# Smaller pieces of w_in, prepared two steps ahead, in a float32 Fourier-mixing and hard-swish kernel

## The chip, the cores and the metric

The kernel runs on one core of a Trainium2 chip. The metric is the device time of one execution in microseconds (us). The kernel before takes 1949.23 us, the median of 5 runs (1947.43 to 1950.19).

The engines that matter are TensorE (PE: matrix products, and PEld: its weight loads), VectorE (DVE), ScalarE (ACT), GpSimd (POOL) and SyncE (SP). Each works through its own queue of instructions in order; they wait for each other through semaphores. POOL and SP also issue the transfers (DMAs).

## The reference

```
X = fft(x, axis=1); X = fft(X, axis=2); x = X.real    # x: 8 x 3008 x 256, float32
x = x.reshape(24064, 256)
h = x @ w_in                                           # w_in: 256 x 2048
g = h * clip(h + 3, 0, 6) / 6                          # hard swish
out = g @ w_out                                        # w_out: 2048 x 256
```

The inputs w_in and w_out arrive as 64-bit floats; the rest is float32.

## The kernel before

The eight batches are worked on in pairs. Stage 1 (`stage1_first` for the first pair) transforms along one factor of the sequence (3008 = 47 x 64) and sends its result to DRAM (`zd`); `load_g` brings it back as g, turned; stage 2 (`stage2`, and `spread` for one odd column) makes the tile q from it with the tables T. The second transform, along the 256 columns, is not done on q: it is folded into w_in, once, at the start. `fold_w_in` multiplies w_in by the transform's table C and leaves the result in W1 (with one row of it spread over all partitions as the columns of WN).

What follows is a long loop of steps, `steps`, numbered s. A step is a chunk of 256 columns of q times two of the 16 blocks of 128 hidden columns: blocks fc and fc + 8, so eight steps (fc = 0 to 7) make a chunk. A step consists of

- `mlp1`: the products u and v (PE, eight passes of 256 columns; four matmuls, of which each is two passes in float32), then s = u + qn * WN, u = s + v, v = v - s (DVE), two ReLUs (ACT) and two gates (DVE), which leave the tile a;
- `combine` (POOL): four sums of a's quarters, for a fast matrix scheme of seven products instead of eight;
- `mlp2`: the products with w_out's blocks G into the accumulators acc, fourteen passes. For the first chunk (s = 0 to 7) `mlp2_first` uses the plain eight products instead, of twice the length in four matmuls (eight passes of 512 columns), since G's mixed blocks aren't made yet.

The loop is in software pipeline order: u and v of step s + 1 (s + 2 from step 8 on) are issued before the products with w_out of step s. The tiles u and v come from one pool of three buffers (`ps_h`, tag "uv"), so the v of a step can start only when DVE has finished with the u of the step before.

The weights are prepared beside the first steps. They come in 16 pieces j of 128 x 512 numbers, loaded by POOL (`load_w`; the 64-bit numbers are read as integers). ACT cuts the exponent out (`exponent_a`, two instructions into PM), PE subtracts its two halves with a product in float16 (`exponent_b`, tile ex, two passes), ACT scales it (`exponent_c`); DVE makes the mantissa (`mantissa`, two instructions into top) and multiplies both (`join`, into wi for w_in, into G for w_out). The functions `head` (exponent_a, mantissa and the next load), `tail` (exponent_c and join) and `unit` group these.

The order of all this is written out by hand: what stands first in the program stands first in each engine's queue. Before the loop, pieces 0 to 3 (all of w_in that the first two steps need) are prepared and half of their columns folded; between the first u and v and the next, the other half is folded (`fold_now(0, 1)`, `fold_now(NWI // 2, 1)`). Pieces 4 to 7 are w_out's for steps 0 to 3; pieces 8 to 11 are the rest of w_in, 12 to 15 the rest of w_out. `third_step` and `fourth_step` (s = 2 and 3) carry pieces 8 to 14, and four half-folds, with them; DUE puts pieces 6, 7, 14 and 15 behind steps 0, 1, 4 and 5. Each w_in fold is eight passes of 256 columns on PE, an ACT copy to W1, and, for its column of WN, either eight tiny products (`pw`) and a copy, or two DMAs of 128 numbers each on SP's queue (line 659).

Of the kernel before, what the change touches and what calls it, by code (L numbers as in the profile page):

```python
# [58 lines left out]
def kernel(  # L59
# [149 lines left out]
    def bank(shape, name):  # L209
        if starting[0]:  # L210
            return ps_a.tile(shape, F32, tag="acc", name=name)
        return ps_d.tile(shape, F32, tag="d", name=name)
# [154 lines left out]
                    self.blocks[m][4:] = [(m, 0), (2 + m, 0)]  # L367

    def mlp1(ch, fc):
        gr, of, nq = ch.ck // 2, ch.ck % 2 * TB, ch.nq  # L370
        q, qn = ch.pr.q[gr], ch.pr.qn[gr]
        u = ps_h.tile([P, 2, TB], F32, tag="uv", name="u")
        v = ps_h.tile([P, 2, TB], F32, tag="uv", name="v")
        for blk, ps in ((0, u), (1, v)):

            r = slice(0, P - blk)
            for i in range(2):
                f = fc + i * NF
                nc.tensor.matmul(ps[:, i, 0:nq], W1[r, blk, f * P:(f + 1) * P], q[r, blk, of:of + nq],  # L379
                                 start=True, stop=True)  # L380
        s = spool.tile([P, 2, TB], F32, tag="s", name="s")
        for i in range(2):
            f = fc + i * NF
            nc.vector.scalar_tensor_tensor(s[:, i, 0:nq], qn[:, of:of + nq], WN[:, f:f + 1], u[:, i, 0:nq],  # L384
                                           op0=AL.mult, op1=AL.add)


        a = apool.tile([P, 2, 2, TB], F32, tag="a", name="a")
        t = spool.tile([P, 2, 2, TB], F32, tag="t", name="t")
        ch.a[fc] = a  # L390
        if ch.last:
            activate_last(a, t, s, u, v, nq)
            return
        nc.vector.tensor_tensor(u[:], s[:], v[:], op=AL.add)  # L394
        relu(t[:, 0], u[:], 1.0 / 6.0)
        nc.vector.tensor_tensor(v[:], v[:], s[:], op=AL.subtract)  # L396
        relu(t[:, 1], v[:], -1.0 / 6.0)
        gate(a[:, 0], t[:, 0], u[:])
        rev, tk, vk = (m.rearrange("p i (k n) -> p (i k) n", n=N2) for m in (a[:, 1], t[:, 1], v[:]))
        gate(rev[:, :, ::-1], tk, vk)  # L400
# [38 lines left out]

    def mlp2_first(ch, fc):
        a = ch.a.pop(fc)
        for h in range(2):
            if fc == 0:
                ch.acc[h] = ps_a.tile([P, 2, TB], F32, tag="acc", name="acc")
            for f in range(2):
                nc.tensor.matmul(ch.acc[h][:], G[:, (B11, B12, B21, B22)[2 * f + h], fc, :], a[:, :, f],  # L448
                                 start=(fc == 0 and f == 0), stop=(fc == NF - 1 and f == 1))
        if fc == NF - 1:  # L450
            ch.r = epool.tile([P, 2, 2, TB], F32, tag="r", name="r")
            for h in range(2):
                for m in range(2):
                    nc.scalar.mul(ch.r[:, m, h], ch.acc[h][:, m], (1 - 2 * m) / WS)

# [86 lines left out]

    NWI, NWO = FF // 512, NF // 2
    WB = 512
    PIECES = [("in", 0), ("in", NWI // 2), ("out", 0), ("out", 1), ("in", 1), ("in", NWI // 2 + 1)]
    PIECES = [(k, n, i) for k, n in PIECES + [("out", j) for j in range(2, NWO)] for i in range(2)]
    assert NWI == 4 and NWO == 4
    raw, difs, exs, fracs, w = {}, {}, {}, {}, {}  # L550

    STRAIGHT = (0, 1, 8, 9, 14, 15)
    NEXT = {0: 8, 1: 9, 4: 10, 5: 11, 6: 12, 7: 13, 8: 14, 9: 15}

    def load_w(j):
        kind, n, i = PIECES[j]
# [2 lines left out]
        st = pool.tile([P, 2 * WB], I32, tag=tag, bufs=bufs, name="st")  # L559
        o = st[:].bitcast(moe_w_in.dtype)  # L560
        if kind == "in":
            nc.gpsimd.dma_start(out=o, in_=moe_w_in[i * P:(i + 1) * P, n * WB:(n + 1) * WB])
        else:
            r = (2 * n + i * NF) * P
            nc.gpsimd.dma_start(out=o.rearrange("p (c j) -> p c j", c=2),
# [16 lines left out]

    def exponent_b(j):
        pm = [PM[j % len(PM)][:, i].bitcast(F16) for i in range(2)]
        if j in (5, len(PIECES) - 1):
            exs[j] = wpool.tile([P, WB], F32, tag="ex", bufs=2, name="ex")
            nc.vector.tensor_tensor(exs[j][:], pm[0], pm[1], op=AL.subtract)
            return

        h = starting[0] or (j % 2 == 0 and 8 <= j < 14)  # L590
        exs[j] = ps_h.tile([P, WB], F32, tag="uv", name="ex") if h else bank([P, WB], "ex")
        for i in range(2):
            nc.tensor.matmul(exs[j][:], E[:, i], pm[i], start=(i == 0), stop=(i == 1))

    def exponent_c(j):
        nc.scalar.activation(exs[j][:].bitcast(I32), exs[j][:], AF.Identity, scale=2.0 ** 23)

    def mantissa(j):
        st = raw.pop(j)
# [7 lines left out]

    def join(j):
        kind, n, i = PIECES[j]
        frac, ex = fracs.pop(j), exs.pop(j)[:]  # L610
        if kind == "in":
            o = wpool.tile([P, WB], F32, tag="wi", bufs=4, name="wi")
            nc.vector.tensor_tensor(o[:], frac, ex, op=AL.mult)
# [10 lines left out]
    def mix_w_out(j):  # L624
# [5 lines left out]
        tt(g[5], g[B22], g[3], op=AL.add)  # L630
        tt(g[2], g[5], g[B21], op=AL.subtract)


    def fold_w_in(n, h):

        nb = WB // 2
        cs = slice(n * WB + h * nb, n * WB + (h + 1) * nb)

        ps = bank([P, 2, nb], "wps") if starting[0] else spare[len(copies) % 2]
        for blk in range(2):  # L640
            for i in range(2):
                nc.tensor.matmul(ps[:, blk], C[:, i, blk * P:(blk + 1) * P],  # L642
                                 w["in", n, i][:, h * nb:(h + 1) * nb], start=(i == 0), stop=(i == 1))
        fs = range(cs.start // P, cs.stop // P)


        pw = ps_h.tile([P, nb // P], F32, tag="uv", name="pw") if h == 0 else None
        for f in fs if h == 0 else ():
            for i in range(2):
                nc.tensor.matmul(pw[:, f - fs[0]:f - fs[0] + 1], w["in", n, i][:, (f % (WB // P)) * P:(f % (WB // P) + 1) * P],  # L650
                                 C[:, i, D - 1:D], start=(i == 0), stop=(i == 1))

        def copy():
            nc.scalar.copy(W1[:, :, cs], ps[:])
            if pw is not None:
                nc.scalar.copy(WN[:, fs[0]:fs[-1] + 1], pw[:])
                return
            for f in fs:
                nc.sync.dma_start(out=WN[:, f:f + 1], in_=W1[P - 1:P, 1, f * P:(f + 1) * P])

        copies.append(copy)

    def load_t(gr):
        for b in range(2):
# [29 lines left out]
        t = T[r, b].rearrange("p g a k n -> p g (a k n)")  # L694
        nc.scalar.copy(t, Z[r].unsqueeze(1).to_broadcast([N2, NG, 2 * TB]))

    copies = []

    def head(j):
        exponent_a(j)
# [8 lines left out]
        exponent_c(j)  # L711
        join(j)

    def unit(j):
        exponent_b(j)
        if j + 1 < len(PIECES):
            head(j + 1)
        tail(j)

    def fold_now(n, *hs):  # L720
        for h in hs:
            fold_w_in(n, h)

    def copy_all():
        while copies:
            copies.pop(0)()


    def see(x):
        nc.gpsimd.tensor_copy(seen[:], x)  # L730
# [5 lines left out]
    for k, c in enumerate(ORDER):  # L736
        for part in range(2):
            fold(first, c, part, nc.vector)
        stage1_first(first, c)
        keep_awake(1)  # L740
        if k + 3 < NXC:
# [14 lines left out]
    for j in range(4, 8):  # L756
        load_w(j)

    head(0)
    exponent_b(0)  # L760
    keep_awake(1)
    head(1)
    tail(0)
    exponent_b(1)
    keep_awake(1)
    head(2)
    tail(1)
    exponent_b(2)
    fold_now(0, 0)
    head(3)  # L770
    tail(2)
    exponent_b(3)
    copy_all()
    tail(3)
    for i in range(2):
        stage2(first, 0, i)
    spread(first, 0)
    fold_now(NWI // 2, 0)
    copy_all()
    starting[0] = False  # L780
    spare = [ps_a.tile([P, 2, WB // 2], F32, tag="acc", name="spare") for h in range(2)]

# [52 lines left out]
        p, ck, fc = steps[s]  # L835
        return chunks[p][ck], fc


    DUE = [(6,), (7,), (), (), (14,), (15,), (), ()]
    head(4)  # L840
    mlp1(*chunk(0))
    exponent_b(4)
    head(5)
    tail(4)
    fold_now(0, 1)
    fold_now(NWI // 2, 1)
    copy_all()
    unit(5)


    def third_step():
        exponent_a(9)
        mlp1(*chunk(3))
        exponent_b(8)
        mlp2_first(*chunk(2))
        tail(8)
        head_b(9)
        exponent_b(9)
        tail(9)

    def fourth_step():
        mlp2_first(*chunk(3))
        head(10)
        head(11)
        exponent_b(10)
        exponent_b(11)
        fold_now(1, 0)
        tail(10)
        tail(11)
        head(12)  # L870
        head(13)
        copy_all()
        exponent_b(12)
        exponent_b(13)
        fold_now(NWI // 2 + 1, 0)
        tail(12)
        tail(13)
        copy_all()
        mlp1(*chunk(4))
        fold_now(1, 1)  # L880
        fold_now(NWI // 2 + 1, 1)
        head(14)
        copy_all()

    prev = None
    for s, (p, ck, fc) in enumerate(steps):
# [3 lines left out]
            f(*a)  # L890
        if s < NF:

            if s in (2, 3):
                (third_step if s == 2 else fourth_step)()
            else:
                mlp1(*chunk(s + 1))
                if s == NF - 1:
                    combine(*chunk(NF))
                mlp2_first(*chunk(s))
            for dst, src in later[2 * s:2 * s + 2]:  # L900
                nc.sync.dma_start(out=dst, in_=src)
            for j in DUE[s]:
                unit(j)

            if s == 5:
                see(chunk(s + 1)[0].a[s + 1][:, 0, 0, 0:1])
                mix_w_out(0)
                mix_w_out(1)
            if s == NF - 1:
                mlp1(*chunk(NF + 1))  # L910
        else:
            if s + AHEAD < len(steps):
                mlp1(*chunk(s + AHEAD))
# [99 lines left out]
```

## Time and profile before

| | |
|---|---|
| median of 5 runs | 1949.23 us |
| profiled execution, its time | 1948.63 us |
| its span | 1946.7 us |
| PE busy | 1927.9 us (99%) |
| PEld busy | 1658.0 us (85%) |
| DVE busy | 1439.2 us (74%) |
| POOL busy | 1416.1 us (73%) |
| ACT busy | 682.5 us (35%) |
| first u of the loop (line 379) | starts at 51.11 us |
| first product of mlp2 (line 468, s = 8) | starts at 119.55 us |

The span is the time from the first to the last instruction of the profiled execution. "Busy" is the time that at least one instruction of the engine is on record; for PE, whose matmuls overlap, a busy share of 99% does not exclude short waits. A row of the timeline gives the start, the length, the engine, the line, the operation, out<-in, the shapes and how many; what stands in brackets is the engine's idle time before it and what ended it. In the trace a matmul of float32 shows as two passes.

### The profile page before, as it was taken

What the parts mean: (1) busy time and instruction counts of PE and PEld (TensorE: products, weight loads), DVE (VectorE), ACT (ScalarE), POOL (GpSimd) and SP (SyncE); (2) the same over time, 40 slices, a digit from 0 to 9 for tenths busy, and PEclk for the clock granted to TensorE, in tenths of its full rate; (3) what the DMA queues carried; (4) which work ended last, traced back from release to release, by engine and by line L of the source; (5) the groups of instructions that cost most, each with busy time, mean ns of one, the idle gap of its engine ahead of it and who ended that gap; (6) DMA issues with size and microseconds to landing.
All of it is one profiled execution on the core that took longest, in us unless ns stands there. A gap on an engine that the chain in (4) does not pass through costs nothing.

```text
span 1946.7 us, 27925 instructions
## 1 busy us (share of the span) xinstructions
PE 1927.9 (99%) x9254; PEld 1658.0 (85%) x9254; DVE 1439.2 (74%) x2778; ACT 682.5 (35%) x1166; POOL 1416.1 (73%) x1620
## 2 busy tenths in 40 slices
PE   8999999999999999999999999999999999999998
PEld 4678888888998888888898888888899888888887
DVE  6877777777777777777787777777778777777777
ACT  5633333333333333333333333333333333333332
POOL 3078888887688887787678887878667667666765
PEclk9999999999999999999999999999999999999999
DMA  8531312211112132111111221222110101101000
GB/s 225 173 87 39 75 52 59 55 43 31 37 30 55 47 76 63 43 51 30 39 36 44 57 55 44 49 51 53 35 28 20 28 17 26 35 12 28 19 19 20
DMA packets 148959, 96.71 MB, mean 50 GB/s; under 512 B 117791, under 2 KB 131235, under 8 KB 148814
## 3 DMA queue, kind: packets, MB, share of 16 engines
q1 hardware_dynamic: 137482, 58.09, 12.5%
q0 software_dynamic: 10672, 36.67, 6.7%
q8 instruction: 73, 1.20, 0.3%
q14 instruction: 72, 0.59, 0.1%
q10 hardware_dynamic: 660, 0.16, 0.0%
HBM read 57.57 MB, written 37.32 MB: 49 GB/s over the span
## 4 chain that ended last, share of the span: by engine, by line
PE 93%; DVE 3%; DMA 1%; ACT 1%; issue 1%; SPq 0%; DVEq 0%; POOL 0%; ACTq 0%
PE acc L468 56%; PE v L379 16%; PE u L379 16%; PE ps L328 2%; PE ps L223 1%; DMA xt<-in_x_dram,IX 1%; DVE a L424 1%; PE acc L448 1%; DVE s L384 1%; ACT t L421 1%; PE spare L642 0%; DVE o L529 0%; DVE u L405 0%; ACT PM L581 0%; DMA T<-in_c_stage_dram 0%
## 5 line engine op out<-in xcount | busy, mean ns | idle before, releaser
L438 POOL TENSOR_TENSOR c<-a 128x512 f32<-128x512 f32 (+1 forms) x375 | 469.1, 1251 | 363.4 <-PE acc L468 307.4
L468 PE MATMUL acc<-c,G 128*128 128x256 f32 (+1 forms) x3008 | 696.9, 374 | 0.0
L421 ACT ACTIVATE t<-u,half 128x512 f32<-128x512 f32 (+1 forms) x384 | 260.8, 679 | 1143.2 <-DVE u L394 1064.2
L468 PEld LDWEIGHTS acc<-c,G 128*128 128x128 f32 x3008 | 565.4, 190 | 71.1
L384 DVE SCALAR_TENSOR_TENSOR s<-qn,WN,u 128x256 f32<-128x256 f32 (+1 forms) x768 | 330.4, 471 | 333.0 <-PE u L379 332.2
L468 PE MATMUL acc<-a,G 128*128 128x256 f32 (+1 forms) x2256 | 541.2, 375 | 0.0
L468 PEld LDWEIGHTS acc<-a,G 128*128 128x128 f32 x2256 | 421.4, 189 | 71.2 <-issue 17.6
L379 PE MATMUL v<-q,W 127*128 127x256 f32 (+1 forms) x1536 | 389.0, 375 | 2.4 <-DVE a L424 2.4
L379 PE MATMUL u<-q,W 128*128 128x256 f32 (+1 forms) x1536 | 388.1, 375 | 0.0
L424 DVE SCALAR_TENSOR_TENSOR a<-t,u 128x512 f32<-128x512 f32 (+2 forms) x448 | 264.0, 601 | 103.0 <-ACT t L421 98.9
L379 PEld LDWEIGHTS v<-q,W 127*128 127x128 f32 x1536 | 288.2, 190 | 42.2 <-DVE a L424 1.9
L379 PEld LDWEIGHTS u<-q,W 128*128 128x128 f32 x1536 | 285.7, 190 | 35.2 <-issue 0.5
L438 POOL TENSOR_TENSOR c<-a,c 128x256 f32<-128x256 f32 (+1 forms) x375 | 269.2, 718 | 29.4
L438 POOL TENSOR_TENSOR c<-c,a 128x256 f32<-128x256 f32 (+1 forms) x375 | 268.9, 717 | 29.4
L394 DVE TENSOR_TENSOR u<-s,v 128x512 f32<-128x512 f32 x352 | 245.0, 696 | 38.1 <-DVE s L384 1.8
L424 DVE SCALAR_TENSOR_TENSOR a<-t,v 128x512 f32<-128x512 f32 (+1 forms) x480 | 263.8, 566 | 0.2
L421 ACT ACTIVATE t<-v,half 128x512 f32<-128x512 f32 (+1 forms) x384 | 260.7, 679 | 0.6 <-PE acc L468 0.4
L396 DVE TENSOR_TENSOR v<-v,s 128x512 f32<-128x512 f32 x352 | 243.9, 693 | 0.0
L438 POOL TENSOR_TENSOR r<-w,e 128x256 f32<-128x256 f32 (+1 forms) x92 | 88.8, 987 | 3.6
L478 ACT ACTIVATE e<-acc 128x512 f32<-128x512 f32 (+2 forms) x184 | 83.4, 545 | 0.0
L529 DVE STREAM_TRANSPOSE o<-r 128x256 f32<-128x256 f32 (+1 forms) x192 | 72.5, 415 | 0.2
L438 POOL TENSOR_TENSOR w<-w,e 128x512 f32<-128x512 f32 (+1 forms) x46 | 57.5, 1251 | 3.6
(103 smaller groups left out, 777.8 us busy)
## 6 DMA issues: line engine op xcount, KB each, us to landing
out_dram<-o SPq DMA_DIRECT2D x747, 32.0 KB
zd<-z SPq DMA_DIRECT2D x48, 192.0 KB
g<-zd SPq DMA_DIRECT2D x36, 256.0 KB
xt<-in_x_dram POOLq DMA_DIRECT2D x21, 256.0 KB, 3.7
qn<-qd SPq DMA_DIRECT2D x19, 256.0 KB
st<-in_moe_w_in_dram POOLq DMA_DIRECT2D x8, 512.0 KB, 8.7
st<-in_moe_w_out_dram POOLq DMA_DIRECT2D x8, 512.0 KB, 6.0
xt<-in_x_dram POOLq DMA_DIRECT2D x17, 192.0 KB, 4.0
```

Of the source, the lines that this page charges most:

```text
L223: nc.tensor.matmul(ps[b][h * PB:(h + 1) * PB, 0:n], F[rows(b), 0:PB], y[rows(b), 2 * h:2 * h + n], start=True, stop=not last, skip_group_c ...
L328: nc.tensor.matmul(ps[:, blk, u * P:n].rearrange("p (b k) -> p b k", b=2), g[:, kk, blk * (P + 1):blk * (P + 1) + P], T[:, :, gr, blk, kk, ...
L379: nc.tensor.matmul(ps[:, i, 0:nq], W1[r, blk, f * P:(f + 1) * P], q[r, blk, of:of + nq], start=True, stop=True)
L384: nc.vector.scalar_tensor_tensor(s[:, i, 0:nq], qn[:, of:of + nq], WN[:, f:f + 1], u[:, i, 0:nq], op0=AL.mult, op1=AL.add)
L394: nc.vector.tensor_tensor(u[:], s[:], v[:], op=AL.add)
L396: nc.vector.tensor_tensor(v[:], v[:], s[:], op=AL.subtract)
L421: nc.scalar.activation(t, h, AF.Relu, bias=half[:], scale=scale)
L424: nc.vector.scalar_tensor_tensor(dst, t, 1.0, h, op0=AL.min, op1=AL.mult)
L438: (eng or nc.gpsimd).tensor_tensor(out, in0, in1, op=AL.add)
L468: nc.tensor.matmul(ch.acc[i // 2][:, i % 2, 0:ch.n], G[:, i, fc, :], mv, start=(fc == 0 and i % 2 == 0), stop=(fc == NF - 1), skip_group_c ...
L478: nc.scalar.mul(ch.e[:, k:i + 1, 0:ch.n], ch.acc[i // 2][:, 0:i + 1 - k, 0:ch.n], 1.0 / WS)
L529: nc.vector.transpose(o[:, 0:n // DH, h], ch.r[:, m, h, 0:n].rearrange("p (j i) -> p j i", i=DH))
```

## The change

The pieces of w_in become 256 columns wide, with both halves of the 256 rows in one piece (128 x 2 x 256), where they were 512 columns of one half. So one piece is enough for one fold, and four pieces (two of w_in, two of w_out) hold all that two steps need. The order of the pieces becomes in, in, out, out, four times.

Before the loop only two pieces of w_in are folded, one with `pw` and one with DMAs into WN; pieces 2 and 3 (w_out's first) have their exponents subtracted by DVE instead of PE; the first `exponent_a` stands ahead of the last `stage1_first`. In the loop `first_steps` (even s) and `second_steps` (odd s) replace the hand-written third and fourth step and DUE: steps 0, 2 and 4 each begin the preparation of the next four pieces and fold two of them, steps 1, 3 and 5 finish it. All later folds use DMAs for WN. `mlp1` is split into its products and `activate`; `mlp2_first` takes a list of halves, and half of each odd step's products with w_out (four of eight passes) stands behind the next step's u and v. Exponents of odd pieces are kept in the banks `spare` that the folds also use.

```diff
-    NWI, NWO = FF // 512, NF // 2
+    NWI, NWO = FF // 256, NF // 2
     WB = 512
-    PIECES = [("in", 0), ("in", NWI // 2), ("out", 0), ("out", 1), ("in", 1), ("in", NWI // 2 + 1)]
-    PIECES = [(k, n, i) for k, n in PIECES + [("out", j) for j in range(2, NWO)] for i in range(2)]
+    PIECES = [q for j in range(NWO) for q in [("in", j, 0), ("in", j, 1), ("out", j, 0), ("out", j, 1)]]
...
-    def mlp2_first(ch, fc):
-        a = ch.a.pop(fc)
-        for h in range(2):
+    def mlp2_first(ch, fc, halves=(0, 1)):
+        a = ch.a[fc]
+        for h in halves:
...
-        if j in (5, len(PIECES) - 1):
+        if j in (2, 3):
...
+        if starting[0]:
+            exs[j] = ps_h.tile([P, WB], F32, tag="uv", name="ex")[:]
+        elif j % 2 == 0:
+            exs[j] = bank([P, WB], "ex")[:]
+        else:
+            exs[j] = spare[1 if j % 4 == 1 else 0][:].rearrange("p i n -> p (i n)")
...
-    def fold_w_in(n, h):
+    def fold_w_in(j, spread_by_pe=False):
...
+        nc.scalar.copy(W1[:, :, cs], ps[:])
+        if pw is not None:
+            nc.scalar.copy(WN[:, fs[0]:fs[-1] + 1], pw[:])
+            return
+        for f in fs:
+            nc.sync.dma_start(out=WN[:, f:f + 1], in_=W1[P - 1:P, 1, f * P:(f + 1) * P])
...
+        if k == NXC - 1:
+            exponent_a(0)
         stage1_first(first, c)
...
-    head(0)
+    head_b(0)
     exponent_b(0)
     keep_awake(1)
+    exponent_c(0)
     head(1)
-    tail(0)
+    join(0)
+    keep_awake(1)
     exponent_b(1)
-    keep_awake(1)
-    head(2)
     tail(1)
+    exponent_a(2)
+    fold_w_in(0)
+    head_b(2)
     exponent_b(2)
-    fold_now(0, 0)
-    head(3)
+    exponent_a(3)
+    fold_w_in(1, spread_by_pe=True)
+    head_b(3)
+    exponent_b(3)
     tail(2)
-    exponent_b(3)
-    copy_all()
     tail(3)
     for i in range(2):
         stage2(first, 0, i)
     spread(first, 0)
-    fold_now(NWI // 2, 0)
-    copy_all()
...
+    exponent_a(4)
     mlp1(*chunk(0))
+    head_b(4)
+    head(5)
...
+    def first_steps(s):
+        j = 2 * s + 4
+        more = j < len(PIECES)
+        if s > 0:
+            mlp2_first(*chunk(s - 1), halves=(1,))
+        if more:
+            exponent_b(j)
+        uv = mlp1_products(*chunk(s + 1)) if s == 0 else None
+        if more:
+            exponent_b(j + 1)
+            tail(j)
+            tail(j + 1)
+            exponent_a(j + 2)
+        activate(*chunk(s + 1), *(uv or mlp1_products(*chunk(s + 1))))
+        mlp2_first(*chunk(s))
+        if more:
+            exponent_b(j + 2)
+            exponent_c(j + 2)
+            exponent_a(j + 3)
+            fold_w_in(j)
+            fold_w_in(j + 1)
+            exponent_b(j + 3)
+
+    def second_steps(s):
+        j = 2 * s + 4
+        if j - 2 < len(PIECES):
+            head_b(j)
+            join(j)
+            head_b(j + 1)
+            exponent_c(j + 1)
+            if j + 2 < len(PIECES):
+                head(j + 2)
+            join(j + 1)
+            if j + 3 < len(PIECES):
+                head(j + 3)
+            mlp2_first(*chunk(s), halves=(0,))
+            mlp1(*chunk(s + 1))
+            return
+        mlp1(*chunk(s + 1))
+        combine(*chunk(s + 1))
+        mlp2_first(*chunk(s), halves=(0,))
+        mlp1(*chunk(s + 2))
+        mlp2_first(*chunk(s), halves=(1,))
```

## The prediction

> **What bounds the kernel now.** I read the page first, then busy time by stretches, the chain of waits over the start, and the timeline from 37 to 121 us, since the diff touches nothing behind that. The page:
>
> ```profile
> span 1946.7 us, 27925 instructions
> ...
> PE 1927.9 (99%) x9254; PEld 1658.0 (85%) x9254; DVE 1439.2 (74%) x2778; ACT 682.5 (35%) x1166; POOL 1416.1 (73%) x1620
> ...
> PEclk9999999999999999999999999999999999999999
> ...
> PE 93%; DVE 3%; DMA 1%; ACT 1%; issue 1%; SPq 0%; DVEq 0%; POOL 0%; ACTq 0%
> ```
>
> PE bounds the whole, at full clock. By stretches (length, then busy time of PE, PEld, DVE, ACT, POOL, the clock, DMA share and GB/s):
>
> ```profile
> 51.10:66.30 15.20, 14.27 (x57) 10.00 (x57) 12.81 (x26) 10.59 (x18) 2.00 (x4) 1.00 0.83 274
> 66.30:81.80 15.50, 15.26 (x51) 8.04 (x49) 14.44 (x28) 11.58 (x19) 1.95 (x3) 1.00 0.67 206
> ...
> 120.00:196.00 76.00, 76.00 (x367) 66.19 (x366) 55.60 (x100) 24.39 (x41) 65.34 (x76) 1.00 0.19 48
> ```
>
> From 120 us on PE never waits; so whatever brings the first product of line 468 forward brings the end forward by as much. Before that PE does wait, and DVE is nearly as full. The chain of waits before the first u, then the timeline:
>
> ```profile
> 46.06 1.78 PE ps L328 x16
> 47.84 0.89 PE ps L339 x8
> 48.74 1.73 PE wps L642 x8
> 50.47 0.79 PE pw L650 x8
> ```
>
> ```profile
> 51.11 1.11 PE L379 MATMUL u<-q,W 128*128 128x256 f32 x4
> ...
> 60.49 2.84 PE L448 MATMUL acc<-a,G 128*128 128x512 f32 x6 [0.93 <-DVE G L619]
> ...
> 118.58 1.13 PE L379 MATMUL v<-q,W 127*128 127x256 f32 x4 [1.54 <-DVE a L424]
> ...
> 119.55 1.46 PE L468 MATMUL acc<-a,G 128*128 128x256 f32 x6
> ```
>
> The reader is to see: after stage 2 (lines 328, 339) PE still folds for 2.5 us before u; w_out's products wait for G at 60.49; and v waits at 118.58, as three uv buffers are in use. So the start has two parts: the time to the first u (51.11), and from there to line 468 (68.44).
>
> **Part A, up to the first u.** PE's last stage-1 work ends at 37.67 (the two passes of awake at 36.81, 0.43 each). Before, piece 0's PM begins on ACT only at 37.50, behind the last copies of z. After, it stands ahead of them; piece 0 lands at 33.28, ACT needs 0.70 each, and is free by 34.4, so PM is ready at 35.9, and the copy that waits for PE at 36.16 isn't held. On PE then: ex 0 (0.43) to 38.1; two awakes (0.86 each) to 39.8; ex 1 waits for its PM (ACT: exponent_c 0.59 from 38.3, PM 1.40 to 40.3) and ends at 40.6; two folds, 16 passes of 0.2155, 3.45, to 44.0; pw 0.81 to 44.85; stage 2 16 passes 1.78 and spread 0.89 (rows above) to 47.5, if g is there: it was at 44.69, and the stores and SP's issues ahead of it are unchanged. ACT in the same time: PM of pieces 2 and 3, copies 0.59 and 0.16, two exponent_c 0.60 each to 46.65, q's copy 0.59 to 47.25; it does not hold u. DVE's two added subtractions (0.68) lie beside the folds. First u: 47.5 for 51.11, **3.6 us** earlier. Ends: 2.5 (only fold and pw behind stage 2 vanish) and 4.0.
>
> **Part B, from u to line 468, work.** Before, in PE start-to-start times: eleven u and v pairs by 1.725 = 18.98; eight w_out steps by 3.435 = 27.48; ten exponents by 0.43 = 4.30; 48 fold passes = 10.36; two pw = 1.62; one half of stage 2 0.89. Sum 63.63 of 68.44, which leaves 4.81 of waits: 1.20 at 60.49, 0.52 at 75.63, 0.71 at 83.6 and 84.0 (exponents), 0.37 at 105.5, 1.82 at 118.58, 0.18 at two u. After: no pw (-1.62), two exponents more (pieces 5 and 15 went by DVE; +0.86): 62.87, **0.76 us** less. Splitting step s's products in two costs nothing: the same passes, other place.
>
> **Part B, waits.** The 4.81 have mostly no counterpart: G for step 0 is joined at about 47.6, 6 us before its use, at 53.75; half of step 7's products lie ahead of the u and v that waited 1.82. What is late next:
> - Piece 4. POOL issues it behind `seen`, as before (45.23), and the first piece then landed at 49.18. PM takes 1.40, to 50.65; PE has finished v at 49.2, and its ex needs 0.43: it waits 1.25. Behind this PM on ACT stand step 0's ReLUs, behind them DVE's gate (0.69, to 52.05), and the second v, which needs that u's buffer: 0.4. Piece 5's PM stands behind the ReLUs: 0.3. Later pieces have more than 6 us of slack.
> - Bank `spare`: the exponent of piece 7 needs the copy of the first fold, which stands on ACT behind a PM (1.40): 0.4.
> - WN by SP. After each pair of folds SP issues four DMAs, 0.6 each, ahead of the stores to zd and loads of T, which queue behind them now. SP has the time: one zd store took up to 2.56 us to issue and one load of T 1.79, but all that SP issued between 60.2 and 71.7 fits between two pairs of folds, 16 us apart. DVE's s of the next step is the instruction that waits; the rest of its activation is queued behind it on DVE, and ACT's ReLUs and two steps' products wait for that. The trace's semaphore records give the landing of such writes: 3.9 to 4.8 us after issue for the four at 57.67, beside loads of pieces; 2.0 to 3.1 for the four at 92.70, with none. For the first pair my count goes: u of step 2 at 63.6 on PE, the w_out half, two exponents and u of step 3 behind it, so PE wants the v of step 3 at 68.8. The first fold's copy ends at 61.4; the first write lands 4.84 later, at 66.25 (the third, which s also needs, 1.2 + 3.9 later); s to the release of u took 3.1 (93.01 to 96.13), so v starts at 69.35: 0.5. Later pairs have no loads beside them (pieces 14 and 15 are issued at about 64 and 65) and I take 2.5, which costs nothing. If all four of a set are equally late, the third decides, some 3.7 us are free and each us beyond costs one: 4.8 in all three sets, the slowest row, would cost 3.3.
>
> Sum 2.85, with 0.15 for single gaps of 0.1 **3.0 us** for 4.81: 1.8 less. Ends: 1.0 (piece 4 lands 1 us earlier, WN in 2.5) and 7.8 (pieces 2 us later, +2; WN at 4.8 in all three sets, 3.3 for 0.5).
>
> One rule speaks against this choice. The rows are the two sets of four just given. Of the Trainium skill, the page "DMA: Bandwidth & Descriptors" says in "Rules for kernel authors" that many small transfers should be coalesced, as under 64 KB it is mostly overhead that is paid; and "Anatomy of one DMA" has a fixed part of some 2.0 us. The change adds six DMAs of 512 B in the place of products. By the fixed 2.0 us, an estimate from that page, no set would cost anything: waits of 2.5, and 1942.5 us; by the slow row in every set it would be 1945.8. The trace agrees with the 2.0 only where no loads run.
>
> **Covers.** For two steps DVE has four mantissas (1.15 each), two joins of w_in (0.61), four of G (0.38), two activations (3.4 each): 14.1 us, against PE's 15.8 (2 x 1.725 + 2 x 3.435 + 4 x 0.43 + 3.45). ACT has 11.8. If DVE's work grew by 1.7 us a pair of steps, it would be the bound. POOL: the mixes of G run from 102.33 to 109.4, combine at 114.04; after, `seen` is released at about 99.5, so they end at 106.6, and combine's a comes at 109.5: covered. w_in's pieces have two rows of 2 KB per partition in place of one of 4 KB, like w_out's: 0.72 to issue for 0.54, four times ahead of the stage that waits, in the ends above.
>
> **Sum.** 3.6 + 0.76 + 1.8 = 6.2 us: line 468 starts at 113.3, the span is 1940.5. The profiled execution took 1948.63 for its 1946.7 (1.9 around it), the median of the runs is 0.6 above it: 1949.2 - 6.2 = **1943.0 us**.
>
> **Rivals.**
> - WN late (the other side). If the writes land 6 us after issue in all three sets, 3 x 2.3 = 6.9 less the 0.5 counted eats the gain: 1949.4; from 7.3 us on it is slower by 0.2% (1953.2). For it: SP's queue fills there, and 4.8 has been seen. Against: 2.0 to 3.1 without loads. Chance 0.06. A part of it, 4.8 everywhere (1945.8; 1947.8 with the pieces 2 us late as well): 0.08.
> - DVE becomes the bound in steps 0 to 5. For: 14.44 of 15.50 busy already; and at 104.52 two G joins took 1.84 for 0.75 while POOL mixed G. Were all four of a pair so slow, +2.2, DVE would need 16.3 for PE's 15.8; with one wait for PE more, 0.5, it is 1 us for each of three pairs: 1946.0. Against: POOL has nothing but loads to issue then. 0.10.
> - The gain is given back: something behind 120 us (POOL's combine, x's loads) keeps its time. 1948 to 1949.5. Against: PE's 76.00 of 76.00, and everything there is placed by steps. 0.06.
> - The forecast, waits of 1 to 4.5 us: 1941.0 to 1944.6. 0.70.
>
> **How the numbers follow.** 0.2% is 3.9 us, about what a measurement of this kernel can tell from no change; faster means below 1945.3. The forecast's 0.70 is faster, and half of the 0.18 of the two partial rivals, where only one or two of the three places are hit: 0.79. The other half and the gain given back: 0.15. Slower: 0.06. The range takes the forecast's low end and the partial rivals: 1940.8 to 1946.4.
>
> **What would show it.** Right: first u at 47 to 48, line 468 at 112 to 114.5, no pw but one, waits of PE on ACT's PM at 50 and of v on DVE's a at 69, none over 0.5 us at 112. Wrong: DVE's s waiting for a DMA to WN and PE for a in three places; PE idle before acc with DVE without a gap; line 468 early but the end not.

## The result and the profile after

| | before | after |
|---|---|---|
| median | 1948.0 us (48 runs, 1946.17 to 1952.73) | 1944.37 us (28 runs, 1941.83 to 1948.98) |
| ratio | | 0.9981, 95% interval 0.9976 to 0.9986 |
| profiled execution, its time / span | 1948.63 / 1946.7 us | 1943.18 / 1941.4 us |

The change saves 3.7 us (2.7 to 4.7 by the interval); the forecast was a saving of 6.2. The predicted time, 1943.0, lies 1.4 under the measured one; but it was counted from a median of 1949.23, and the larger set puts the kernel before at 1948.0.

The page after, the lines that answer to those shown of before:

```profile
span 1941.4 us, 27877 instructions
...
PE 1925.3 (99%) x9230; PEld 1656.0 (85%) x9230; DVE 1437.4 (74%) x2778; ACT 681.8 (35%) x1163; POOL 1417.3 (73%) x1620
...
PEclk9999999999999999999999999999999999999999
...
PE 94%; DVE 3%; DMA 2%; ACT 1%; issue 0%; POOL 0%; DVEq 0%; SPq 0%; ACTq 0%; POOLq 0%
```

PE is still the bound at full clock, with 24 passes fewer. The stretches after (length, busy time of PE, PEld, DVE, ACT, POOL, clock, DMA share, GB/s):

```profile
46.92:62.73 15.81, 14.54 (x54) 9.04 (x53) 13.66 (x26) 12.39 (x21) 4.30 (x7) 1.00 0.75 264
62.73:79.72 16.99, 15.77 (x57) 9.81 (x56) 14.78 (x30) 11.15 (x19) 1.88 (x3) 1.00 0.61 209
79.72:95.23 15.51, 15.51 (x58) 9.89 (x56) 12.66 (x24) 10.29 (x17) 0.00 (x0) 1.00 0.41 119
120.00:196.00 76.00, 76.00 (x370) 65.23 (x369) 55.17 (x100) 26.79 (x47) 66.19 (x77) 1.00 0.24 58
```

A pair of steps that also prepares weights takes 15.51 us of pure PE work (third line). The two pairs before it lose 1.27 and 1.22 us of PE. The timeline after names where:

```profile
46.92 1.03 PE L381 MATMUL u<-q,W 128*128 128x256 f32 x4
...
48.70 1.40 ACT L591 ACTIVATE PM<-st,bias 128x512 uint8<-128x512 int16 x2 [0.99 <-DMA st<-in_moe_w_in_dram]
...
49.51 0.38 PE L608 MATMUL ex<-PM,E 128*128 128x512 f16 x1 [0.69 <-ACT PM L591]
50.16 0.38 PE L608 MATMUL ex<-PM,E 128*128 128x512 f16 x1 [0.27 <-ACT PM L591]
...
60.58 0.59 PE L608 MATMUL spare<-PM,E 128*128 128x512 f16 x2 [0.25 <-ACT W L668]
...
66.51 0.48 DVE L390 SCALAR_TENSOR_TENSOR s<-qn,WN,u 128x256 f32<-128x256 f32 x1 [1.40 <-DMA WN<-W]
...
69.29 1.13 PE L381 MATMUL v<-q,W 127*128 127x256 f32 x4 [1.22 <-DVE a L430]
...
112.74 1.13 PE L381 MATMUL v<-q,W 127*128 127x256 f32 x4
113.71 1.03 PE L474 MATMUL acc<-a,G 128*128 128x256 f32 x4
```

First the exponent of piece 4 waits at 49.51 (ACT's PM had itself waited 0.99 for the piece), then the exponent of piece 7 at 60.58 (its bank, behind a fold's copy), then v at 69.29, behind a DVE that stood 1.40 us waiting for a write to WN. The wait of v at the end (118.58 before) has shrunk to 0.14. (This is start to start: from the start of one pass to that of the next, less what a pass takes when nothing waits. By this count a wait is some 0.16 us longer than the idle time in its brackets.)

An execution's whole time hides part of this, because the last product of stage 1 (line 278, plus 0.43 for its pass) ends at another time in every execution, as the loads of x land: 35.0 to 37.9 us in all profiles here but one. So I read three stretches, each from PE's starts: from the end of stage 1 to the first u, from there to the first product of mlp2 (line 474, 468 before), and from there to the end.

| kernel | stage 1 to u | u to mlp2 | mlp2 to end | median us | ratio (95%) |
|---|---|---|---|---|---|
| before, two profiles | 14.30, 14.31 | 68.44, 68.45 | 1827.17, 1827.19 | 1948.0 | |
| after | 10.68 | 66.79 | 1827.71 | 1944.37 | 0.9981 (0.9976 to 0.9986) |
| after_again | 11.18 | 66.66 | 1827.71 | 1944.86 | 0.9978 (0.9969 to 0.9987) |
| after_third | 10.84 | 66.50 | 1827.70 | 1944.11 | 0.9976 (0.9965 to 0.9986) |
| whole_steps | 11.14 | 70.77 | 1827.69 | 1946.93 | 0.9994 (0.9985 to 1.0003) |
| exponent0_back | 11.71 | 66.46 | 1827.68 | 1944.07 | 0.9981 (0.9972 to 0.9990) |
| need_order | 11.44 | 67.41 | 1827.70 | 1943.85, one run | |
| late_writes | 11.43 | 75.11 | 1827.34 | 1951.55 | 1.0019 (1.0009 to 1.0028) |
| first_columns_by_pe | 10.91 | 65.98 | 1827.36 | 1942.35, one run | |
| loads_before_seen | 12.89 | 66.92 | 1827.69 | 1944.83, one run | |
| first_columns_timed | 11.10 | 65.81 | 1827.34 | 1942.74 | 0.9966 (0.9952 to 0.9979) |
| third_column_by_pe | 11.16 | 65.14 | 1827.74 | 1942.47 | 0.9967 (0.9955 to 0.9979) |
| more_on_dve | 10.68 | 66.47 | 1827.23 | 1943.86, one run | |

By the means of the three profiles of the changed kernel (10.90, 66.65, 1827.71): 3.4 us saved before the first u, 1.8 from u to mlp2, 0.5 given back behind it: 4.7 us in all. The three comparisons by runs gave 3.7, 4.3 and 4.7.

### The profile page after: what moved, and what is told of

It is laid out like the page before. It is cut to its first block, busy times and chain, and to the rows that moved or that the text cites. A ratio compares the mean times of both kernels' runs of the same rounds, so it can differ in the third digit from the quotient of the medians.

```text
span 1941.4 us, 27877 instructions
## 1 busy us (share of the span) xinstructions
PE 1925.3 (99%) x9230; PEld 1656.0 (85%) x9230; DVE 1437.4 (74%) x2778; ACT 681.8 (35%) x1163; POOL 1417.3 (73%) x1620
## 4 chain that ended last, share of the span: by engine, by line
PE 94%; DVE 3%; DMA 2%; ACT 1%; issue 0%; POOL 0%; DVEq 0%; SPq 0%; ACTq 0%; POOLq 0%
PE acc L474 56%; PE v L381 16%; PE u L381 16%; PE ps L328 2%; PE ps L223 1%; PE acc L454 1%; DMA xt<-in_x_dram,IX 1%; DVE a L430 1%; DVE s L390 0%; ACT t L427 0%; DVE o L535 0%; DVE u L411 0%; PE spare L658 0%; DMA WN<-W 0%; DMA st<-in_moe_w_in_dram 0%
```

## The experiments

**The same kernels again.** after_again and after_third are the changed kernel, before_again the kernel before, without an edit.

> The changed kernel once more, for a second profile. The profiles say 5.3 us for the change (spans 1946.7 and 1941.4), the medians of the runs 3.6. Theory A (the sum of the prediction, of which the profile shows line 474 at 113.7 for 119.55): the runs give -3.5 to -5.5 us again, and the new profile has the first u 9.1 to 11 us behind the end of stage 1's last awake and line 474 66 to 67.5 us behind that u. Theory C (what lands late differs from execution to execution, and the profile caught a quick one): the second profile has the writes of WN or the pieces later, line 474 at 115 us or behind it, and says so in DVE's waits for DMA.

> The kernel before, once more, for a second profile and as a zero of the comparison. Theory A: within 0.5 us of the kernel before in the runs; the profile has the first u at 51 to 51.7 and line 468 68 to 69 us behind it. Theory C, that the first profile of before was a slow one: first u or line 468 1 us or more earlier than 51.1 and 119.55.

> The changed kernel again, beside the two that follow, for a comparison on one chip: 3 to 5 us under the kernel before (1944 to 1945.5), first u to first product of mlp2 66.6 to 66.9 us, and 1827.7 from there to the end, with DVE's gap of 0.46 us before the u of line 411 at its place 1347.9 us behind the first product of mlp2.

The places are those of theory A. The first product of mlp2 stands at 115.77 in after_again, which theory C forecast, but 1.7 of the 2.1 us lie in the end of stage 1 (37.93 for 36.24) and 0.5 in a wait for g; no write or piece came later. In before_again the first u stands at 49.80, again for stage 1, which ended at 35.49 instead of 36.81. before_again gave 1947.65 us, ratio 0.9998 (0.9989 to 1.0007): two sets of one kernel agree within the 0.1% of the interval. What is under 1 us can't be settled by medians here; the middle stretch, equal to 0.01 us in the two profiles of before and within 0.3 in three of after, can settle it.

**whole_steps: the products of a step kept whole.** The split that the prediction costed at nothing is undone; all else stays.

```diff
     def first_steps(s):
-        if s > 0:
-            mlp2_first(*chunk(s - 1), halves=(1,))
...
-            mlp2_first(*chunk(s), halves=(0,))
+            mlp2_first(*chunk(s))
             mlp1(*chunk(s + 1))
```

> The changed kernel with the products of w_out of every step kept together, ahead of the next step's u and v; pieces, folds and their order as after. The split moves 1.72 us of PE work (four passes of 512 columns) between a step's v and the use of what hangs on it. Theory A, in which I costed the split at nothing by itself but let it cover the u and v of steps 8 to 10, and DVE's and ACT's work beside odd steps: without it PE waits about 1 to 1.5 us in each of steps 1, 3, 5 and 7, together 3.5 to 4.5 us slower than after, that is about as fast as before. Theory B (the pieces and the shorter way to the first u carry the gain, the split is decoration): within 1 us of after.

Measured: 1946.93 us, and 70.77 us from u to mlp2, 4.1 more than the mean of after. PE's waits in the timeline of whole_steps, behind the places where after waits too:

```profile
85.04 1.13 PE L381 MATMUL v<-q,W 127*128 127x256 f32 x4 [0.61 <-DVE a L430]
101.43 1.13 PE L381 MATMUL v<-q,W 127*128 127x256 f32 x4 [1.48 <-DVE a L430]
116.18 1.13 PE L381 MATMUL v<-q,W 127*128 127x256 f32 x4 [1.54 <-DVE a L430]
```

Two pairs of u and v follow each other there with no w_out products between them, and the second v wants the buffer that DVE frees 3 us after it begins; start to start the three waits cost 0.78, 1.64 and 1.70. So half a step of products is the cover that these v need: the passes as such cost nothing, their place is worth 4.1 us, most of the 4.7 that the change brings by the stretches; the medians beside each other, 1946.93 and 1944.86 (after_again), show 2.1 of it. Theory A had the size, with four places where the trace has three. Two of the three waits have no counterpart in the kernel before: they belong to the order of the steps that the change itself brings, and the split covers them.

**exponent0_back: the first exponent behind stage 1 again.**

```diff
-        if k == NXC - 1:
-            exponent_a(0)
         stage1_first(first, c)
...
+    exponent_a(0)
     head_b(0)
```

> The changed kernel with the first cutting of an exponent put back behind the last copies of stage 1 on ScalarE. Theory A, Part A of the prediction: PM of piece 0 takes 1.40 us on ScalarE, and PE waits for it, less what awake passes hide: the first u 1.1 to 1.3 us later, and all of it carried to the end: 0.9 to 1.3 us slower than after. Rival: the first u waits for g (landed at 43.9 in the profile of after, where PE came to stage 2 at 44.16): then only what goes beyond g's landing counts, still 1.0. If something behind absorbs it (the wait for piece 4, 1.3 us in the profile of after, shrinks by the same), no change at the end: 0 to 0.3.

Measured: the first u comes 0.8 us later than the mean of after (11.71 behind stage 1), the middle stretch is 0.2 shorter, and the time is the changed kernel's, 1944.07. The first u and v in the timeline of exponent0_back:

```profile
48.97 0.79 PE L608 MATMUL ex<-PM,E 128*128 128x512 f16 x2
49.60 1.02 PE L381 MATMUL u<-q,W 128*128 128x256 f32 x4
51.61 1.13 PE L381 MATMUL v<-q,W 127*128 127x256 f32 x4 [0.98 <-DVE a L430]
```

The exponent of piece 4 no longer waits for its piece, but the second v waits for DVE in its place: start to start 1.45 us of waits remain up to the exponent of piece 5, of 1.61 in after (and the same 1.45 remain in loads_before_seen below). So the wait for piece 4 stands over one that is nearly as long, and an earlier piece alone would bring about 0.2. The earlier exponent is worth 0.8 before the first u, less than the 1.1 to 1.3 expected, and 0.6 in all, which medians don't show.

**need_order: the order of the writes to WN.**

```diff
-        for f in fs:
-            nc.sync.dma_start(out=WN[:, f:f + 1], ...)
+        if k == 1:
+            for f in (fs[0] - NF, fs[0], fs[1] - NF, fs[1]):
+                nc.sync.dma_start(out=WN[:, f:f + 1], ...)
```

> The four writes of a set go to WN in the order in which they are needed: the two columns of the next step (f and f + 8) first, then those of the step behind it. In the trace of the changed kernel the third write was issued at 61.72 us, DVE's s waited 1.40 us for it, and PE's v 1.39 us for DVE. Theory A (the third write of the first set is what v of step 3 waits for, a term that the prediction had at 0.5): the write that decides becomes the second, issued at about 61.1, so v waits about 0.8 in place of 1.39 and the stretch from the first u to the first product of mlp2 is 66.1 to 66.3 us (66.79 and 66.66 in the two profiles of the changed kernel). Rival B (all four land together, beside the loads, whatever their order): 66.6 to 66.8.

Measured: 67.41 us, over both expectations. The write that decides was issued at 61.01 instead of 61.72 (0.42 us earlier, counted from the first u), but DVE waited longer. The two halves of step 2's s, which reads the first two columns of this set, in the timeline of need_order:

```profile
64.57 0.48 DVE L390 SCALAR_TENSOR_TENSOR s<-qn,WN,u 128x256 f32<-128x256 f32 x1
66.86 0.48 DVE L390 SCALAR_TENSOR_TENSOR s<-qn,WN,u 128x256 f32<-128x256 f32 x1 [1.81 <-DMA WN<-W]
```

From issue to the s that it released the write took 5.85 us; the third writes of the three profiles of the changed kernel took 4.79, 4.56 and 4.45. Theory A falls here, and B's size is too small.

The semaphore records in the traces, from which the prediction read its landings, say why. In the ten profiles whose first fold leaves both columns to DMA, the write of this first set that SP issues first lands 1.92 to 1.96 us after its issue (in late_writes it is one into the unread tile); every later one of the set takes 4.43 to 7.58. In after the DMA share is 0.01 from 59.7 to 61.9 us and 0.83 from there to 66.5: the first write, issued at 60.56, is through at 62.49, and the others go out into the loads of the next pieces. The second place, to which this edit moved the column, is one of the late ones. That the loads are what holds the writes is read from these times; no run moves the loads away.

**late_writes: the same writes some 2.4 us later, in all three sets.**

```diff
+        if not starting[0] and k == 0:
+            for i in range(4):
+                nc.sync.dma_start(out=junk[:, i:i + 1], in_=W1[P - 2:P - 1, 1, cs.start:cs.start + P])
         for f in fs:
             nc.sync.dma_start(out=WN[:, f:f + 1], ...)
```

> Ahead of each later set of writes to WN, SP issues four more transfers of 512 B into a tile that nobody reads: the writes go out about 2.4 us later, three times. It leaves nothing out. Theory A (the prediction's count: the third write decides, the first set has no slack left, the other two have little, and beyond it a microsecond is a microsecond): 2.4 us at the first set; at the second, 78.39 + 2.4 + 2.3 to land, s 1.9 later than in the changed kernel, of which about 1.2 reach v; at the third about 1.8. Together 4.5 to 5.4 us: first u to first product of mlp2 71.3 to 72.2 us for 66.8, and a time like that of the kernel before, 1948 to 1950 us, DVE's s waiting for DMA in three places. Rival B (only the first set is near the path, the other two are hidden): 2.0 to 2.8 us, 69.0 to 69.5, and about 1947. Rival C (SP's queue is off the path): under 0.5 us.

Measured: 1951.55 us, slower than the kernel before (1.0019), and 75.11 us, 8.5 more than after. DVE's s that waits for the third write and the v of steps 3, 5 and 7 in its timeline, then the stretches around the first of them (columns as above):

```profile
70.36 0.48 DVE L390 SCALAR_TENSOR_TENSOR s<-qn,WN,u 128x256 f32<-128x256 f32 x1 [1.38 <-DMA WN<-W]
...
73.14 1.22 PE L381 MATMUL v<-q,W 127*128 127x256 f32 x2 [4.80 <-DVE a L430]
...
88.95 0.48 DVE L390 SCALAR_TENSOR_TENSOR s<-qn,WN,u 128x256 f32<-128x256 f32 x1 [0.73 <-DMA WN<-W]
...
91.73 1.13 PE L381 MATMUL v<-q,W 127*128 127x256 f32 x4 [0.28 <-DVE a L430]
...
105.04 0.48 DVE L390 SCALAR_TENSOR_TENSOR s<-qn,WN,u 128x256 f32<-128x256 f32 x1 [0.75 <-DMA WN<-W]
...
107.82 1.13 PE L381 MATMUL v<-q,W 127*128 127x256 f32 x4 [1.18 <-DVE a L430]
```

```profile
68.50:72.00 3.50, 0.00 (x0) 0.00 (x0) 2.01 (x4) 0.32 (x1) 0.00 (x0) 0.92 1.03 363
72.00:74.50 2.50, 1.36 (x3) 1.17 (x4) 2.35 (x5) 2.50 (x5) 0.00 (x0) 0.50 0.86 284
74.50:78.40 3.90, 3.90 (x7) 1.73 (x6) 3.64 (x7) 2.17 (x4) 0.00 (x0) 0.52 0.06 22
78.40:82.00 3.60, 3.60 (x14) 2.25 (x13) 1.94 (x6) 1.29 (x3) 0.00 (x0) 1.00 0.00 0
```

Start to start the three waits are 4.97, 0.44 and 1.35 us, against 1.19 (mean), 0 and 0 in after: 5.6 us, at all three places. That is theory A, a little over its 5.4, since the first set's third write went out 3.75 us later and not 2.4; B and C fall. Another 2.5 us are something else: after 4.80 us without work PE's clock was granted at half, and the passes up to 78.4 took twice their time. Of the remaining 0.4, 0.2 lies in the wait for piece 4.

The 3.7 us that the prediction called free, counted from the issue of a set's third write, nearly hold. In the first set of the three profiles of the changed kernel that write landed 4.77, 4.53 and 4.43 us after its issue and v waited 1.38, 1.15 and 1.05: 3.4 were free each time. In the two later sets of late_writes it landed 4.2 us behind the fold's second copy, right behind which it is issued in after, and v waited 0.44 and 1.35: 3.7 and 2.9 were free. But a quiet write takes 2.0 of them itself, and so little is left that some 2.4 us of SP's queue, lost three times, turn this change's gain into a loss, with the clock's 2.5 on top.

The trace also gives the landing at both loads of the queues, as the time from a write's issue to the s that waited for it. In the first set (DMA share 0.94, 298 GB/s) the two writes that s waited for took 5.23 and 4.89 us; in the other two (share 0.10, 1 GB/s) 2.15, 2.01, 2.16 and 2.05.

**first_columns_by_pe and first_columns_timed: two columns of WN by PE.** One edit in two runs. (The expectations name step 3 as the reader of these columns; it is step 2's activation that reads them, and v of step 3 that waits for the buffer it frees.)

```diff
-            for f in range(2):
+            for f in range(2 if starting[0] else 1):
...
+        if pw is not None:
+            nc.scalar.copy(WN[:, fs[0]:fs[0] + 1], pw[:, 0:1])
+            fs = fs[1:]
...
-            fold_w_in(j)
-            fold_w_in(j + 1)
+            fold_w_in(j, spread_by_pe=(s == 0))
+            fold_w_in(j + 1, spread_by_pe=(s == 0))
```

> The two columns of WN that step 3's activation needs first are made by PE with four tiny passes each, as in the kernel before, only in the first set of folds in the loop; the other columns go by DMA. Theory A (v of step 3 waits 1.39 us for nothing but these writes): that wait goes, PE works 0.8 us more: first u to first product of mlp2 66.1 to 66.4 us for 66.79 and 66.66. Rival B (behind the writes DVE's own work holds v nearly as long, for it is 14 us of every 16 busy): the wait stays over 0.7 us and the stretch becomes 67.0 to 67.6.

> The kernel of first_columns_by_pe, timed: the first two columns that step 3 needs by PE, the rest by DMA. Theory A (the wait for WN was 0.7 to 0.8 us of PE's time net of the eight tiny passes): first u to first product of mlp2 65.9 to 66.1 us, 0.6 to 1.0 us under the changed kernel in the median, and 0.36 more if DVE's gap far behind is absent again: 1.0 to 1.3 under it, about 1943.3. Rival B (one profile's luck): within 0.3 us of the changed kernel.

Measured: 65.98 and 65.81 us, and 1942.74 us. The wait at v is gone and 0.8 us of tiny passes are paid for it: the net 0.75 is theory A's size. Nothing else holds v there. The sum has one more term, though: the wait for the bank of piece 7's exponent (0.41, start to start) is gone too, as tiny passes now stand ahead of it.

**third_column_by_pe: only the column that was late.**

```diff
-            fold_w_in(j, spread_by_pe=(s == 0))
+            fold_w_in(j)
             fold_w_in(j + 1, spread_by_pe=(s == 0))
```

> Only the third column of the first set (f + 8, which the second half of step 3's s needs first) is made by PE, with four tiny passes; the column f goes by DMA as in the changed kernel, where it was issued at 60.56 and s did not wait for it at 64.64. Theory A (the write that was late is the third alone): no wait for WN, 0.4 us of PE's work less than in first_columns_by_pe: first u to first product of mlp2 65.5 to 65.7 us, 1.1 to 1.6 us under the changed kernel. Rival B (the first write is on its edge too, it lands up to 5 us after its issue beside the loads): s waits for it up to 1 us at 64.6, the stretch is 65.9 to 66.6.

Measured: 65.14 us, 1.5 under the mean of after, and 1942.47 us. DVE in the timeline of third_column_by_pe, steps 2 and 3:

```profile
63.90 0.87 DVE L390 SCALAR_TENSOR_TENSOR s<-qn,WN,u 128x256 f32<-128x256 f32 x2
68.78 0.87 DVE L390 SCALAR_TENSOR_TENSOR s<-qn,WN,u 128x256 f32<-128x256 f32 x2
```

No s waits for WN, and the four tiny passes stand where PE waited 0.41 us (start to start, in after) for the bank of piece 7's exponent, a wait that is gone too. Some 0.2 of the 1.5 is not the edit's: piece 4 happened to be waited for 0.67 us here, for 0.85 to 0.94 in the three profiles of after. This version is 6.2 us under before by medians and 1.6 under the changed kernel beside it. The two intervals (0.9955 to 0.9979 and 0.9965 to 0.9986) overlap, so that last step is carried by the stretches, which are those of one profile.

**loads_before_seen: pieces 4 and 5 loaded ahead of the wait for g.**

```diff
+    load_w(4)
+    load_w(5)
     see(first.g[0][:, 0, 0:1])
-    for j in range(4, 8):
+    for j in range(6, 8):
         load_w(j)
```

> POOL issues the loads of pieces 4 and 5 ahead of the instruction that waits for g, in place of behind it. In the changed kernel the exponent of piece 4 and v behind it cost PE 0.86 + 0.43 us of waiting at 49 us, as ACT waited 0.99 us for the piece. Theory A (the wait is the late issue's and nothing else): first u at its place behind stage 1 (10.7 to 11.2 us behind the end of stage 1's products), and from the first u to the first product of mlp2 65.4 to 65.8 us for 66.79. Rival B (the megabyte of the two pieces shares the queues with z's way to DRAM and back, so g comes later): first u 11.7 to 13 us behind stage 1, with PE waiting for g ahead of stage 2, and the sum of both stretches the same as in the changed kernel or longer (77.5 us and more).

Measured: the wait for piece 4 is gone, and the first u comes 2.0 us later; both stretches together take 79.8 us for 77.6. PE in the timeline of loads_before_seen:

```profile
45.56 2.02 PE L328 MATMUL ps<-T,g 128*128 128x128 f32 x16 [2.08 <-DMA WN<-W]
...
52.68 1.13 PE L381 MATMUL v<-q,W 127*128 127x256 f32 x4 [0.98 <-DVE a L430]
```

Stage 2 waits 2.08 us. The profile puts that down to a write of WN, as it does in need_order; but stage 2 reads g, and POOL's own wait for g ended at the same 45.56. That the megabyte of the two pieces slowed g's way is rival B's account, and the times fit it; in this one execution the place of that wait on POOL is one that the changed kernel is right to keep.

**more_on_dve: sixteen memsets at the start.** It asks where the 0.5 us behind the first product of mlp2 went.

```diff
     nc.vector.memset(half[:], 0.5)
+    for i in range(16):
+        nc.vector.memset(idle[:], 0.0)
```

> Sixteen memsets of one column on DVE at the start, where it has nothing to do from 4.4 to 7.8 us; else the changed kernel. In all six profiles with the same 2778 instructions on DVE and the changed order, but not in late_writes and first_columns_by_pe, DVE stood 0.46 us ahead of the u of line 411 that is its instruction 2068, for nothing that the trace names, and PE 0.36 behind it. Theory A (an accident of where the instructions lie in the stream of DVE): the gap is gone or stands at another instruction, and the stretch from the first product of mlp2 to the end is 1827.2 to 1827.4 us, or 1827.7 with the gap elsewhere. Rival B (it belongs to the work at that place: the output's transfers, POOL's combine): it stays before the same u, 1347.9 us behind the first product of mlp2. The start is as in the changed kernel: 66.6 to 66.9 us.

In after, DVE and PE at one place far behind, first DVE then PE's v behind it:

```profile
1462.07 0.57 DVE L411 TENSOR_TENSOR u<-s,v 128x388 f32<-128x388 f32 x1 [0.46 <-DVE s L390]
...
1464.18 0.90 PE L381 MATMUL v<-q,W 127*128 127x194 f32 x4 [0.56 <-DVE a L430]
```

The same two in more_on_dve:

```profile
1462.43 0.57 DVE L411 TENSOR_TENSOR u<-s,v 128x388 f32<-128x388 f32 x1
...
1464.55 0.90 PE L381 MATMUL v<-q,W 127*128 127x194 f32 x4 [0.20 <-DVE a L430]
```

The gap is gone and the stretch is 1827.23 us, as before the change. Work and order at that place are the same in both, so the 0.36 us belong to where instructions lie, not to the work there: theory A. late_writes and both runs of first_columns have no gap either, with DVE's 2778 instructions unchanged in number. But DVE's queue also holds semaphore instructions, whose number the edits change, and counted with these in the traces the u stands behind 2879 others in all eight profiles that have the gap, and behind 2874, 2878, 2880 or 2895 in the six that have none. Why that place costs 0.36 us stays open.

## Why the prediction was right, and where it was off

Of what it said would show it: the first product of mlp2 at 113.71 (forecast 112 to 114.5), PE's waits on PM at 50 and of v on DVE's a at 69, and none over 0.5 at 112 are all in the trace; the first u came at 46.92, just ahead of its 47 to 48.

**Part A (first u 3.6 us earlier): right.** It had the first u 10.7 us behind the end of stage 1; it came at 10.68, 10.84 and 11.18. The condition it named, "if g is there", decides now: its working left PE's work and g 0.16 us apart, and in after_again stage 2 waits for g:

```profile
46.36 2.02 PE L328 MATMUL ps<-T,g 128*128 128x128 f32 x16 [0.37 <-DMA g<-zd]
```

Less work for PE there would hardly bring u forward now.

**Part B, work (0.76 us less): right.** By difference, 66.79 less the forecast's 62.87 leaves 3.92 of waits; ten waits of over 0.06 us, start to start, make 3.84 of it, the rest is smaller ones.

**Part B, waits (3.0 us for 4.81; 3.92 in after): the step that failed.** Start to start in after, against the forecast's terms:

| term | forecast | after |
|---|---|---|
| piece 4, v on u's buffer, piece 5's PM | 1.95 | 1.61 |
| bank `spare` | 0.4 | 0.41 |
| WN by SP, first set | 0.5 | 1.48 |
| WN by SP, the two later sets | 0 | 0 |
| single gaps, v at the end among them | 0.15 | 0.42 |

The mis-sized term is WN's. The mechanism and the place (v of step 3) were right. That the times agree, 69.35 by the forecast and 69.29 in the trace, is in part luck, as the first u came 0.6 earlier than forecast: counted from u, v started at 22.37 for 21.85. The landings were not right: the forecast had the first write land in 4.84 us and the third in 3.9, as in the set at 57.67 of before. Here the first took 1.93, and the third, which decides, 4.77, 4.53 and 4.43. And PE wanted v 20.98 behind u, 0.3 earlier than counted, because the terms ahead of it had come out 0.3 lower: what they saved was waited out at this write. The price, "each us beyond costs one", held in late_writes, and the "3.7 us free" came out at 3.4, 3.7 and 2.9. That the later sets cost nothing held too.

**"Splitting step s's products in two costs nothing: the same passes, other place": true of the passes, and too little said.** The prediction named this half as cover for step 7 alone, worth 1.82. whole_steps shows three such places, worth 4.1 us; that the other two, 2.4 us, hang on it too, the prediction did not say. Its sum is not wrong for that, since the change keeps the split. That DVE's pace then holds PE is near to the rival "DVE becomes the bound"; in the changed kernel it does not occur.

**The gain given back.** The rival (0.06) thought of POOL's combine or x's loads. 0.5 us of it was there in every profile of the changed kernel, but by more_on_dve it is no part of the work that the change moves. "Against: PE's 76.00 of 76.00" could not see it, more than 1200 us further on.

**The base.** The forecast took 6.2 from 1949.23. From 1948.0 it would have been 1941.8, and the miss 2.6: by the three profiles' means 0.2 in part A, 0.8 in the waits, 0.5 behind mlp2, and 1.1 that the runs' interval doesn't resolve. Five runs were a base with more than a microsecond of error.

## What to carry to other kernels

Before costing a reordering at nothing, look at what the moved work stands in front of: here its only value was as cover, and without it 4.1 of the 4.7 us that the stretches show are lost. A small transfer whose reader waits should be priced by landings seen beside the same loads (4.5 to 5.9 us here) and not by quiet ones (2.0 to 2.2); when only one of a set is late, do that one another way. And when one stage comes earlier, ask which transfer it now arrives before.

## What the runs showed of the hardware

**The clock falls after an idle stretch of PE.** In first_columns_timed a late load of x left PE without work for 3.46 us in stage 1 (PE row, then the stretch behind it):

```profile
29.65 0.45 PE L261 MATMUL pt<-y,F 94*96 94x4 f32 x2 [3.46 <-DVE y L195]
```

```profile
29.65:36.20 6.55, 6.55 (x12) 2.97 (x13) 5.45 (x11) 1.49 (x4) 1.44 (x2) 0.54 1.02 291
```

The granted clock was 0.54 over the next 6.5 us. That execution took 1946.4 us where the median of its kernel is 1942.74, so such a stall explains part of the spread of single runs. In after_again 2.57 us of idle ended at 28.81, and a stretch at half clock followed, here the row from its windows; in late_writes 4.80 us came with the half clock shown above.

```profile
29.80:33.20 3.40, 3.40 (x5) 1.23 (x4) 3.30 (x7) 1.17 (x2) 0.60 (x1) 0.50 1.03 317
```

After the idle times of 1.2 to 2.08 us in the other profiles the clock stayed at 1.00. The Trainium skill ("TensorE: Matmul & The Clock Gate", section "Why this matters for your kernels") advises against idle gaps of more than about 3 us between bursts of matmuls; here 2.57 sufficed, in one execution.

**A small transfer's landing more than doubles beside loads.** The Trainium skill's page "DMA: Bandwidth & Descriptors" gives in "Anatomy of one DMA" a fixed part of some 2.0 us, for transfers that GpSimd issues. SP's writes of 512 B agree with it where the queues were quiet: the s that waited for them started 2.01 to 2.16 us after their issue. Beside loads the same 512 B took 4.45 to 5.85, and the write that went out first, before the loads moved, 1.92 to 1.96 in ten profiles.

**0.36 us come and go with the placing of instructions,** 1348 us behind the first product of mlp2, at the same instruction to 0.03 us in all profiles that have it. That is a tenth of this change's effect, and too small to be seen in medians.
